# One score bank per block of an attention kernel exponentiated on GpSimd by pow instead of on ScalarE

## The chip, the cores and the metric

One core of one Trainium2 chip. The metric is the device time of one execution in microseconds. Before: 530.76 us, median of 2 runs (530.7 to 530.82); in later jobs on other chips the same kernel took 527.4 to 533.3, so single runs here carry about half a per cent of noise. A kernel is compared with runs of the kernel before on the same chip; each run also has a state, and only fast runs are compared, except where a kernel had a single run, whose state is unknown.

## The reference, cut to what matters

```python
xn = layernorm(x)                                  # x: 1 x 2048 x 448, bf16
q, k, v = split(xn @ wqkv)                         # 16 heads of 28
p = softmax(q @ k.T * 28 ** -0.5)
s = (p @ v) @ wo
g = silu(gelu(xn @ w1 + b1) @ w2 + b2)
return x + s * g
```

16 heads x 2048 x 2048 scores have to be exponentiated. That is the largest work outside TensorE.

## The kernel before

A small scheduler written in Python places every instruction with an assumed duration and emits one in-order program per engine; semaphores carry the dependences. Scores are made in 16 blocks (4 groups of heads x 4 chunks of queries) of 64 banks of 128x512. Three banks (two in the first block) are exponentiated by one ScalarE instruction. PSUM is where the matmuls of this kernel put their results, SBUF where everything else lies; a bank is one 128x512 tile of scores in PSUM.

```python
UB = 3; NRING = 6; NP = 21
...
def fexp(eng, b0=b0, p0=p0, n=n):                  # p_exps, ScalarE (L932)
    return eng.activation(K.P[:, p0:p0 + n, :], K.ring[:, b0:b0 + n, :], ACTF.Exp, scale=SM_SCALE)
...
# p_pv, TensorE (L969): P and the values, summed over the 64 banks of a block in one PSUM bank
eng.matmul(K.acc[32 * j:32 * j + 32, ...], K.vaug[:, t, 4 * g + j, :], K.P[:, PB[m], ...], ...)
...
# p_silu, VectorE (L871): two SBUF inputs
eng.scalar_tensor_tensor(K.g_sb[:, c, t, :], sg[:, t, :], 1.0, fb[:, t, :], op0=ALU.add, op1=ALU.mult)
```

The ring has six PSUM banks, that is, two units of three: TensorE fills one while ScalarE reads the other. `acc` holds one block at a time, so every bank of a block must have been multiplied in before the block can be closed, some 28.6 us (64/3 x 1.343) after it began.

Of the kernel before, what the change touches and what calls it, by code (L numbers as in the profile page):

```python
# [8 lines left out]
ALU = mybir.AluOpType  # L9
ET = mybir.EngineType  # L10

PE, ACT, DVE, POOL, SP = ET.PE, ET.Activation, ET.DVE, ET.Pool, ET.SP

S = 2048
D = 448
# [12 lines left out]
NBLK = G * C  # L28
MTOT = NBLK * T * 4

UNITS = []
for _m in range(0, 64, 2):
    UNITS.append(([_m, _m + 1], _m % 4, _m % 20))
for _m in range(64, MTOT, UB):
    UNITS.append((list(range(_m, _m + UB)), (_m - 64) % NRING, (_m - 64) % NP))
NU = len(UNITS)
RB = {m: b0 + k for ms, b0, p0 in UNITS for k, m in enumerate(ms)}
PB = {m: p0 + k for ms, b0, p0 in UNITS for k, m in enumerate(ms)}
SM_SCALE = DH ** -0.5
LN_EPS = 1e-5  # L40
KNORM = 2.5
PV_START = 8
SEM = 0.07
EPS = 0.1

# [23 lines left out]
class _Kernel:  # L69
# [19 lines left out]
    def sb(self, name, shape, dtype=dt.bfloat16):  # L89
        return self.es.enter_context(self.nc.sbuf_tensor(name, shape, dtype))  # L90
# [143 lines left out]
    def alloc(self):  # L234
# [57 lines left out]
        self.b_acc, self.b_misc = B(), B()  # L292
        self.b_P = [B() for _ in range(NP)]
        self.b_x = [B() for _ in range(C)]
        self.b_xn = [[B() for _ in range(4)] for _ in range(3)]
        self.b_xnT = [[B(), B()] for _ in range(C)]
        self.b_wqkf = B()
# [24 lines left out]
        self.b_rf = [B(), B()]  # L322
        self.banks = [(self.misc[:, :], self.b_misc), (self.acc[:, :], self.b_acc)]
        self.s_x = [self.sem("s_x%d" % q) for q in range(4)]
        self.s_out = [self.sem("s_out%d" % q) for q in range(10)]
        self.s_w = {n: self.sem("s_" + n) for n in ("wqk", "wv", "w1", "w2", "wo", "b")}

    def schedule(self):
        K = self
        K.n_f1 = 0  # L330
        K.exp_u = -1
        K.sc_u = -1
        K.pv_u = -1
        K.E_done = -1
        K.norms_done = False
        K.stg_done = 0
        K.qsqs = [0, 1]
        K.f2n = [0] * C
        K.pv_started = False
        K.chunks_done = 0  # L340
        K.g_done = [False] * C
        K.on_done = [False] * NBLK
        K.on4 = [False] * 4
        K.ln_done = 0
        K.ring6 = False
        K.taken = 0
        K.ring_busy = [False] * NRING
        K.P_busy = [False] * NP
        K.banks += [(K.ring[:, b, :], K.b_ring[b]) for b in (5, 4)]
        K.outs = []  # L350
        K.b1_done = False
        K.gelu_done = False
        self.constants()
        self.loads()
        for c in range(C):
            K.spawn(K.p_ln(c), c)
        K.spawn(K.p_first(), 0)
        K.spawn(K.p_scores(), 0)
        K.spawn(K.p_take(4), 0)
        K.spawn(K.p_take(5), 0)  # L360
        K.spawn(K.p_exps(), 0)
        K.spawn(K.p_pv(), 0)
        o = 1.0

        def nxt():
            nonlocal o
            o += 1.0
            return o
        K.spawn(K.p_norms(), nxt())
        for c in range(1, C):  # L370
            K.spawn(K.p_tr(c, 0), nxt())
            K.spawn(K.p_tr(c, 1), nxt())
            K.spawn(K.p_k(0, c), nxt())
            if c == 1:
                K.spawn(K.p_v0(0), nxt())
            K.spawn(K.p_v0(c), nxt())
        K.spawn(K.p_q(0, 1), nxt())
        for c in (2, 3):
            K.spawn(K.p_q(0, c), nxt())
        for c in range(C):  # L380
            K.spawn(K.p_k(1, c), nxt())
        K.spawn(K.p_q(1, 0), nxt())
        for t in range(T):
            K.spawn(K.p_v1(t), nxt())
        for c in (1, 2, 3):
            K.spawn(K.p_q(1, c), nxt())
        f1 = deque((c, ft) for c in range(C) for ft in range(FT))
        for c in range(C):
            for _ in range(6):
                K.spawn(K.p_f1(*f1.popleft()), nxt())  # L390
            K.spawn(K.p_k(2, c), nxt())
            K.spawn(K.p_q(2, c), nxt())
        while f1:
            K.spawn(K.p_f1(*f1.popleft()), nxt())
        for c in range(C):
            K.spawn(K.p_k(3, c), nxt())
            K.spawn(K.p_q(3, c), nxt())
        K.spawn(K.p_gelu(), 0)
        for c in range(C):
            for t in range(4):  # L400
                K.spawn(K.p_f2(c, t), nxt())
            K.spawn(K.p_silu(c), nxt())
        K.o_epi = 0.5
        for c in range(C - 1):
            for t in range(4):
                K.spawn(K.p_out(c, t), nxt())
        for t in range(4):
            K.spawn(K.p_last(t), nxt())
        K.run()
        for h in K.outs:  # L410
            K.wait(SP, h)

    def constants(self):
# [3 lines left out]
        def f(eng):  # L417
            eng.memset(K.epsc[:, :], LN_EPS)
            eng.memset(K.dum[:, :], 1.0)
            eng.memset(K.ones[:, :], 1.0)  # L420
            eng.memset(K.E_sb[:, :, :], 0.0)
            eng.memset(K.w1[64:128, 3, :], 0.0)
            eng.memset(K.stg[64:128, 3, :, :, :], 0.0)
            pad = lambda w: w.rearrange("p k (h e) -> p (k h) e", e=32)[:, :, DH:32]
            eng.memset(pad(K.wq[:, :, :]), 0.0)
            eng.memset(pad(K.wk[:, :, :]), 0.0)
            eng.memset(pad(K.wsq), 0.0)
            eng.memset(K.wv[64:128, 3, :], 0.0)
            eng.memset(K.wv[0:64, 3, D:WS], 0.0)
            eng.memset(K.wv[:, 0:3, D:WS], 0.0)  # L430
            return eng.memset(K.xn[:, :, :, D:512], 0.0)
# [432 lines left out]
    def p_silu(self, c):  # L864
        K = self
        yield ("until", lambda: K.f2n[c] == 4 and K.ready([K.b_fsb[c % 2]], 0.3) and (c < 2 or K.g_done[c - 2]))
        fb, sg = K.fsb[:, c % 2, :, :], K.sig[:, c % 2, :, :]
        yield _Task(ACT, lambda eng: eng.activation(sg, fb, ACTF.Tanh, scale=0.5),
                    [K.b_fsb[c % 2]], [K.b_sig[c % 2]], 1.6, 0.0, 0)
        for t in range(4):  # L870
            yield _Task(DVE, lambda eng, t=t: eng.scalar_tensor_tensor(K.g_sb[:, c, t, :], sg[:, t, :], 1.0, fb[:, t, :],  # L871
                                                                       op0=ALU.add, op1=ALU.mult),
                        [K.b_sig[c % 2], K.b_fsb[c % 2]], [K.b_h[c], K.b_g[c]], 0.63, 0.0, 6)
        K.g_done[c] = True

    def pieces(self, m):
        b, r = m // 64, m % 64
# [11 lines left out]
    def p_scores(self):  # L889
        K = self  # L890
        for u in range(NU):
# [23 lines left out]
            if len(ms) == 3 and not K.ring6:  # L915
                yield ("until", lambda: K.taken == 2)
                K.ring6 = True
            yield ("until", lambda: not any(K.ring_busy[RB[m]] for m in ms))
            yield _Task(PE, fall, rd, [K.b_ring[RB[m]] for m in ms], 0.17 + 0.05 * len(ms) + 0.02 * (len(fl) - len(ms)), 0.1, 1)
            for m in ms:  # L920
                K.ring_busy[RB[m]] = True
            K.sc_u = u

    def p_exps(self):
        K = self
        for u in range(NU):
            ms, b0, p0 = UNITS[u]
            n = len(ms)
            yield ("until", lambda: K.sc_u >= u and not any(K.P_busy[p0 + k] for k in range(n)))

            def fexp(eng, b0=b0, p0=p0, n=n):
                return eng.activation(K.P[:, p0:p0 + n, :], K.ring[:, b0:b0 + n, :], ACTF.Exp, scale=SM_SCALE)  # L932
            yield _Task(ACT, fexp, [K.b_ring[b0 + k] for k in range(n)], [K.b_P[p0 + k] for k in range(n)],
                        0.0843 + 0.4267 * n, 0.08, 3)
            for k in range(n):
                K.ring_busy[b0 + k] = False
                K.P_busy[p0 + k] = True
            K.exp_u = u
            if u >= NU - 2:
                for k in range(n):  # L940
                    K.banks.append((K.ring[:, b0 + k, :], K.b_ring[b0 + k]))

    def p_pv(self):
        K = self
# [2 lines left out]
        K.banks.pop(i)  # L947
        K.pv_started = True
        for u in range(NU):
            ms = UNITS[u][0]  # L950
            parts, cur = [], []
            for m in ms:
                cur.append(m)
# [4 lines left out]
            for part in parts:  # L958
                if not part:
                    continue  # L960
                first = K.sub_of(part[0])
                yield ("until", lambda: K.exp_u >= u and K.E_done >= first - 1)
                fl, rd = [], []
                for m in part:
                    b, j, pc, end, s = K.pieces(m)
# [15 lines left out]
                yield _Task(PE, fall, rd, [K.b_acc], 0.18 + 0.05 * len(part) + 0.02 * (len(fl) - len(part)), 0.1,  # L981
                            lambda: 1.2 if K.exp_u - K.pv_u > 4 else 6)
                for m in part:
                    K.P_busy[PB[m]] = False
                if end:
                    K.spawn(K.p_epi(b) if b < NBLK - 1 else K.p_epi4(s), 0.5)
            K.pv_u = u
# [72 lines left out]
    def t_oev(self, ps, tok, c, t):  # L1060
# [2 lines left out]
        wr = K.b_osb[c][t // 2] if c < C - 1 else K.b_o4[t]  # L1063
        yield _Task(DVE, lambda eng: eng.tensor_tensor(o, ps, K.g_sb[:, c, t, :], ALU.mult),  # L1064
                    [tok, K.b_g[c]], [wr], 0.63, 0.0, 3)
        yield _Task(DVE, lambda eng: eng.tensor_tensor(o, o, K.x_sb[:, c, t, :], ALU.add),
                    [K.b_x[c], wr], [wr], 0.4, 0.0, 3)
        ov = K.out[0].rearrange("(c p t) d -> c p t d", p=128, t=4)[c]
        if c == C - 1:
            K.outs.append(K.dma(SP, lambda eng: eng.dma_start(ov[:, t, :], o), K.s_out[6 + t], reads=[wr]))  # L1070
# [75 lines left out]
```

## Time and profile before

| | before |
|---|---|
| time | 530.76 us |
| ScalarE busy | 502.8 us, 95% |
| TensorE busy | 466.3 us, 88% |
| GpSimd busy | 64.1 us, 12% |
| pitch of a three-bank exponential | 1.343 us |

### The profile page before, as it was taken

How to read it: one execution, taken by the hardware profiler on the slowest of the kernel's cores; microseconds unless marked ns; L12 is line 12 of the kernel's file. 1: busy time of each engine (PE TensorE's matmuls, PEld its weight loads, DVE VectorE, ACT ScalarE, POOL GpSimd, SP SyncE). 2: the span in 40 equal slices, each digit the busy share in tenths (PEclk: the TensorE clock that was granted, in tenths of full speed). 3: DMA queues.
4: the chain of work that ended last, by engine and by line, in shares of the span. 5: the costliest groups of instructions: out<-in, count | busy, mean ns of one | idle time of the engine just before them, and what ended most of it. 6: DMA issues, size and time to landing. Idle time of an engine off the chain costs nothing.

```text
span 529.0 us, 8343 instructions
## 1 busy us (share of the span) xinstructions
PE 466.3 (88%) x3478; PEld 149.9 (28%) x3507; DVE 172.5 (33%) x304; ACT 502.8 (95%) x385; POOL 64.1 (12%) x93
## 2 busy tenths in 40 slices
PE   6899899899989999989976799999878889898984
PEld 2433233222222222222221333333212112121542
DVE  6823433343433343343433132313400003031244
ACT  3898999999999999999999799999999999999993
POOL 5662101210101001010111001000101000010100
PEclk9999999999999999999995999999955558566698
DMA  8800000000000000000000000000000000000010
GB/s 238 245 16 18 0 1 1 0 1 1 1 1 1 0 1 2 1 1 1 0 1 0 0 2 1 1 0 1 1 0 2 0 1 35 1 14 22 2 46 27
DMA packets 7925, 9.13 MB, mean 17 GB/s; under 512 B 2384, under 2 KB 6928, under 8 KB 7888
## 3 DMA queue, kind: packets, MB, share of 16 engines
q1 hardware_dynamic: 7888, 8.61, 5.3%
q8 instruction: 27, 0.44, 0.3%
q14 instruction: 10, 0.08, 0.0%
HBM read 6.77 MB, written 1.84 MB: 16 GB/s over the span
## 4 chain that ended last, share of the span: by engine, by line
ACT 44%; PE 36%; issue 14%; DVE 5%; ACTq 0%; DVEq 0%
ACT P L932 44%; PE ring L903 8%; PE misc L854 8%; PE acc L969 7%; PE misc L591 3%; PE misc L1055 2%; PE acc L678 2%; PE misc L771 1%; PE misc L1040 1%; DVE h L1064 1%; DVE qT L747 1%; PE misc L811 1%; DVE qT L757 1%; DVE h L871 1%; PE ring L591 1%
## 5 line engine op out<-in xcount | busy, mean ns | idle before, releaser
L932 ACT ACTIVATE P<-ring 128x1536 bf16<-128x1536 f32 (+1 forms) x352 | 461.8, 1644 | 7.3 <-PE ring L903 4.7
L903 PE MATMUL ring<-qT,kT 32*128 32x512 bf16 (+1 forms) x1216 | 151.4, 386 | 31.7 <-ACT P L932 29.2
L969 PE MATMUL acc<-P,vaug 128*32 128x512 bf16 (+1 forms) x1216 | 145.5, 390 | 0.0
L903 PEld LDWEIGHTS ring<-qT,kT 32*128 32x128 bf16 x1216 | 38.1, 94 | 156.6 <-ACT P L932 132.0
L824 DVE TENSOR_SCALAR h<-misc,b1c 128x512 bf16<-128x512 f32 x56 | 42.0, 751 | 80.4 <-PE misc L811 80.4
L811 PE MATMUL misc<-xnT,w 128*128 128x512 bf16 x209 | 58.8, 382 | 3.3 <-issue 1.3
L969 PEld LDWEIGHTS acc<-P,vaug 128*32 128x32 bf16 x1216 | 35.6, 96 | 83.5 <-issue 80.6
L854 PE MATMUL misc<-w,h 128*128 128x448 bf16 x224 | 52.5, 362 | 3.7 <-DVE qT L757 2.0
L1030 POOL CAST rhi<-rc 128x512 bf16<-128x512 f32 x15 | 9.1, 609 | 306.6 <-DVE rc L1026 223.8
L1016 DVE CAST E_sb<-acc 128x512 bf16<-128x512 f32 x15 | 10.3, 687 | 79.6 <-PE acc L969 79.6
L752 POOL TENSOR_TENSOR qsq<-qT 128x512 bf16<-128x512 bf16 x15 | 15.6, 1039 | 113.1 <-DVE qT L747 113.1
L859 DVE TENSOR_TENSOR w<-misc,b2b 128x448 bf16<-128x448 f32 x16 | 10.0, 622 | 54.3 <-PE misc L854 54.3
L854 PEld LDWEIGHTS misc<-w,h 128*128 128x128 bf16 x224 | 18.1, 99 | 28.4 <-issue 11.3
L836 ACT ACTIVATE h<-h 128x7168 bf16<-128x7168 bf16 x4 | 24.4, 6163 | 0.0
L811 PEld LDWEIGHTS misc<-xnT,w 128*128 128x128 bf16 x224 | 15.5, 97 | 30.2 <-issue 9.6
L591 PE MATMUL misc<-xnT,wq 128*128 128x512 bf16 x53 | 15.7, 418 | 3.0 <-DVE qT L757 2.5
L591 PE MATMUL misc<-xnT,wk 128*128 128x512 bf16 x47 | 14.9, 424 | 3.9 <-DVE qT L747 2.8
L1045 DVE TENSOR_TENSOR qT<-misc,E_sb 128x512 bf16<-128x512 f32 x15 | 10.4, 691 | 21.4 <-PE misc L1040 21.4
L747 DVE CAST qT<-misc 128x512 bf16<-128x512 f32 x14 | 9.7, 691 | 20.2 <-PE misc L591 20.2
L1031 POOL TENSOR_TENSOR rlo<-rc,rhi 128x512 bf16<-128x512 f32 x15 | 16.0, 1064 | 1.2
L602 DVE TENSOR_SCALAR kT<-misc,ecol 128x512 bf16<-128x512 f32 x13 | 9.8, 750 | 19.3 <-PE misc L591 19.3
L1055 PE MATMUL misc<-wo,qT 128*128 128x448 bf16 x56 | 15.1, 371 | 0.8 <-DVE w L1004 0.4
(119 smaller groups left out, 245.7 us busy)
## 6 DMA issues: line engine op xcount, KB each, us to landing
x_sb<-in_A_x_dram SPq DMA_DIRECT2D x4, 448.0 KB, 6.7
w<-in_B_w_dram SPq DMA_DIRECT2D x1, 1568.0 KB, 13.0
w<-in_B_w_dram SPq DMA_DIRECT2D x1, 1344.0 KB, 7.5
out_dram<-h SPq DMA_DIRECT2D x6, 224.0 KB, 2.0
h<-in_A_wqkv_dram SPq DMA_DIRECT2D x1, 672.0 KB, 4.8
out_dram<-h SPq DMA_DIRECT2D x4, 112.0 KB, 1.7
wo<-in_A_wo_dram SPq DMA_DIRECT2D x16, 24.5 KB
wv<-in_A_wqkv_dram SPq DMA_DIRECT2D x1, 336.0 KB, 5.7
```

The lines of the kernel that those rows point to most:

```text
L591: ins = eng.matmul(bank, w[:, kt, g * 128:(g + 1) * 128], K.xnT[:, kt, c * 512:(c + 1) * 512], start=(kt == 0), stop=(kt == KT - 1))
L747: yield _Task(DVE, lambda eng: eng.tensor_copy(qb, bank), [tok], [qr], 0.7, 0.0, 2)
L752: yield _Task(POOL, lambda eng: eng.tensor_tensor(qs, qb, qb, ALU.mult), [qr], [tq], 1.05, 0.0, 0)
L811: ins = eng.matmul(bank, K.w1[:, kt, ft * 128:(ft + 1) * 128], K.xnT[:, kt, c * 512:(c + 1) * 512], start=(kt == 0), stop=(kt == KT - 1))
L824: yield _Task(DVE, lambda eng: eng.tensor_scalar(dst, bank, K.b1c[:, ft:ft + 1], None, op0=ALU.add), [tok, K.b_b1c], wr, 0.75, 0.0, 2)
L836: return eng.activation(hv, hv, ACTF.Gelu_apprx_tanh)
L854: ins = eng.matmul(ps, hv[:, ft, t * 128:(t + 1) * 128], K.w2[:, ft, :], start=(ft == 0), stop=(ft == FT - 1))
L903: return eng.matmul(K.ring[:, RB[m], col:col + nq], K.kT[32 * j:32 * j + 32, g, t * 128:(t + 1) * 128], K.qT[32 * j:32 * j + 32, g, c * 51 ...
L932: return eng.activation(K.P[:, p0:p0 + n, :], K.ring[:, b0:b0 + n, :], ACTF.Exp, scale=SM_SCALE)
L969: return eng.matmul(K.acc[32 * j:32 * j + 32, q0:q0 + nq], K.vaug[:, t, 4 * g + j, :], K.P[:, PB[m], col:col + nq], tile_position=(0, 32 * ...
L1031: yield _Task(En, lambda eng: eng.tensor_tensor(K.rlo[:, :, :], rcb, K.rhi[:, :, :], ALU.subtract), [K.b_rc, K.b_rhl], [K.b_rhl], d2, 0.0, 1)
L1055: ins = eng.matmul(ps, K.qT[:, g, c * 512 + t * 128:c * 512 + (t + 1) * 128], K.wo[:, g, :], start=(g == 0), stop=(g == G - 1))
```

## The change

The intent: GpSimd is idle for 88% of the time, and ScalarE is the bound, so one bank of each of the blocks 1 to 14 goes to GpSimd. VectorE first copies the bank, scaled by the softmax scale times log2(e), from PSUM to SBUF in fp32; GpSimd then computes two to the power of it from SBUF. The late bank's matmul is a task of its own, to be placed when the pow has ended. The space of x holds the copies, so x is loaded again for the residual at the end. The core of the diff, cut:

```diff
+LATE = {}
+for _b in range(1, NBLK - 1):
+    for _r in (8,):
+        _m = 64 * _b + _r
+        while (_m - 64) % UB != UB - 1:
+            _m += 1
+        LATE[_m] = POOL
...
+POW_DUR = 20.0
...
+    yield _Task(DVE, lambda eng, m=m, i=i: eng.tensor_scalar(K.ysb[i], K.ring[:, RB[m], :], SM_SCALE * LOG2E,
+                                                             None, op0=ALU.mult), ..., 0.72, 0.0, 1)
...
+    yield _Task(POOL, lambda eng: eng.tensor_tensor(K.plate[k], K.two[:, 0:1].to_broadcast([128, 512]), K.ysb[i],
+                                                    ALU.pow), [K.b_y[i], K.b_pads], [K.b_pl[k]], POW_DUR, 0.0, 2)
...
+    yield ("until", lambda: K.pv_done[64 * b + 3] and K.ready([K.b_pl[k]], 0.1))
+    yield _Task(PE, lambda eng: eng.matmul(K.acc[32 * j:32 * j + 32, :], K.vaug[:, t, 4 * g + j, :], K.plate[k], ...
...
-        yield _Task(DVE, lambda eng: eng.tensor_tensor(o, o, K.x_sb[:, c, t, :], ALU.add),
+        yield _Task(DVE, lambda eng: eng.tensor_tensor(o, o, K.x2[:, c, t, :], ALU.add),
```

In the changed kernel the pow is L998, the scaled copy L988, the late matmul L1004, the exponentials L966, the silu product L904.

More of the change, by code (lines that the diff above doesn't have):

```diff
@@ L29 @@
 MTOT = NBLK * T * 4
-UNITS = []
-for _m in range(0, 64, 2):
-    UNITS.append(([_m, _m + 1], _m % 4, _m % 20))
-for _m in range(64, MTOT, UB):
-    UNITS.append((list(range(_m, _m + UB)), (_m - 64) % NRING, (_m - 64) % NP))
+LATE = {}
[5 more added lines that the diff above has]
+        LATE[_m] = POOL
+UNITS, RB, PB, RPREV, PPREV = [], {}, {}, {}, {}
+_last, _plast, _p = {}, {}, 0
+for _m in list(range(0, 64, 2)) + list(range(64, MTOT, UB)):
+    _ms = list(range(_m, _m + (2 if _m < 64 else UB)))
+    _b0 = _m % 4 if _m < 64 else (_m - 64) % NRING
+    _na = len([m for m in _ms if m not in LATE])
+    if _p + _na > NP:
+        _p = 0
+    UNITS.append((_ms, _ms[:_na], _b0, _p))
+    for _k, m in enumerate(_ms):
+        RB[m] = _b0 + _k
+        RPREV[m] = _last.get(RB[m])
+        _last[RB[m]] = m
+        if _k < _na:
+            PB[m] = _p + _k
+            PPREV[m] = _plast.get(PB[m])
+            _plast[PB[m]] = m
+    _p += _na
 NU = len(UNITS)
-RB = {m: b0 + k for ms, b0, p0 in UNITS for k, m in enumerate(ms)}
-PB = {m: p0 + k for ms, b0, p0 in UNITS for k, m in enumerate(ms)}
 SM_SCALE = DH ** -0.5
+LOG2E = 1.4426950408889634
 LN_EPS = 1e-5
@@ L294, in alloc @@
         self.b_x = [B() for _ in range(C)]
+        self.b_x2 = [B() for _ in range(C)]
+        xf = self.x_sb[:, :, :, :].rearrange("p c t d -> p (c t d)")
+        self.ysb = [xf[:, 1024 * i:1024 * (i + 1)].bitcast(f32) for i in range(2)]
+        self.plate = [xf[:, 2048 + 512 * i:2560 + 512 * i] for i in range(2)]
+        self.x2 = self.h[:, :, 3584:5376].rearrange("p c (t d) -> p c t d", d=D)
+        self.b_y, self.b_pl = [B(), B()], [B(), B()]
+        self.two = sb("two", [128, 1], f32)
         self.b_xn = [[B() for _ in range(4)] for _ in range(3)]
@@ L324, in alloc @@
         self.s_x = [self.sem("s_x%d" % q) for q in range(4)]
+        self.s_x2 = [self.sem("s_x2%d" % q) for q in range(4)]
         self.s_out = [self.sem("s_out%d" % q) for q in range(10)]
@@ L346, in schedule @@
         K.taken = 0
-        K.ring_busy = [False] * NRING
-        K.P_busy = [False] * NP
+        K.ring_rel = [False] * MTOT
+        K.pv_done = [False] * MTOT
+        K.late_left = [len([m for m in LATE if m // 64 == b]) for b in range(NBLK)]
+        K.ys, K.pls = [0, 1], [0, 1]
         K.banks += [(K.ring[:, b, :], K.b_ring[b]) for b in (5, 4)]
@@ L362, in schedule @@
         K.spawn(K.p_pv(), 0)
+        K.spawn(K.p_late(), 0)
         o = 1.0
@@ L419, in f @@
             eng.memset(K.dum[:, :], 1.0)
+            eng.memset(K.two[:, :], 2.0)
             eng.memset(K.ones[:, :], 1.0)
@@ L874, in p_silu @@
         K.g_done[c] = True
+        K.b_x2[c].r = list(K.b_h[c].r) + [K.b_h[c].w]
+        K.dma(SP, lambda eng: eng.dma_start(K.x2[:, c, :, :], K.A_x[0].rearrange("(c p t) d -> c p t d", p=128, t=4)[c]),
+              K.s_x2[c], writes=[K.b_x2[c]])
     def pieces(self, m):
@@ L917, in p_scores @@
                 K.ring6 = True
-            yield ("until", lambda: not any(K.ring_busy[RB[m]] for m in ms))
+            yield ("until", lambda: all(RPREV[m] is None or K.ring_rel[RPREV[m]] for m in ms))
             yield _Task(PE, fall, rd, [K.b_ring[RB[m]] for m in ms], 0.17 + 0.05 * len(ms) + 0.02 * (len(fl) - len(ms)), 0.1, 1)
-            for m in ms:
-                K.ring_busy[RB[m]] = True
             K.sc_u = u
@@ L926, in p_exps @@
         for u in range(NU):
-            ms, b0, p0 = UNITS[u]
+            _, ms, b0, p0 = UNITS[u]
             n = len(ms)
-            yield ("until", lambda: K.sc_u >= u and not any(K.P_busy[p0 + k] for k in range(n)))
+            yield ("until", lambda: K.sc_u >= u and all(PPREV[m] is None or K.pv_done[PPREV[m]] for m in ms))
             def fexp(eng, b0=b0, p0=p0, n=n):
@@ L934, in p_exps @@
                         0.0843 + 0.4267 * n, 0.08, 3)
-            for k in range(n):
-                K.ring_busy[b0 + k] = False
-                K.P_busy[p0 + k] = True
+            for m in ms:
+                K.ring_rel[m] = True
             K.exp_u = u
@@ L941, in p_exps, with p_late, p_pow @@
                     K.banks.append((K.ring[:, b0 + k, :], K.b_ring[b0 + k]))
+    def p_late(self):
+        K = self
+        yield ("until", lambda: K.ln_done == 2 * C)
+        for b in K.b_y + K.b_pl:
+            for x in K.b_x:
+                b.r += x.r
+        for u in range(NU):
+            for m in UNITS[u][0]:
+                if m not in LATE:
+                    continue
+                yield ("until", lambda: K.sc_u >= u and len(K.ys) > 0)
+                i = K.ys.pop(0)
+                yield _Task(DVE, lambda eng, m=m, i=i: eng.tensor_scalar(K.ysb[i], K.ring[:, RB[m], :], SM_SCALE * LOG2E,
+                                                                         None, op0=ALU.mult),
+                            [K.b_ring[RB[m]]], [K.b_y[i]], 0.72, 0.0, 1)
+                K.ring_rel[m] = True
+                K.spawn(K.p_pow(m, i), 0)
+    def p_pow(self, m, i):
+        K = self
+        yield ("until", lambda: len(K.pls) > 0)
+        k = K.pls.pop(0)
+        yield _Task(POOL, lambda eng: eng.tensor_tensor(K.plate[k], K.two[:, 0:1].to_broadcast([128, 512]), K.ysb[i],
+                                                        ALU.pow), [K.b_y[i], K.b_pads], [K.b_pl[k]], POW_DUR, 0.0, 2)
+        K.ys.append(i)
+        b, j, pc, end, s = K.pieces(m)
+        g, t = b // C, pc[0][0]
+        yield ("until", lambda: K.pv_done[64 * b + 3] and K.ready([K.b_pl[k]], 0.1))
+        yield _Task(PE, lambda eng: eng.matmul(K.acc[32 * j:32 * j + 32, :], K.vaug[:, t, 4 * g + j, :], K.plate[k],
+                                               tile_position=(0, 32 * j), start=False, stop=False, skip_group_check=True),
+                    [K.b_pl[k], K.b_v[0 if g == 0 else 1][t]], [K.b_acc], 0.25, 0.1, 1.2)
+        K.pls.append(k)
+        K.late_left[b] -= 1
     def p_pv(self):
@@ L949, in p_pv @@
         for u in range(NU):
-            ms = UNITS[u][0]
+            ms = UNITS[u][1]
             parts, cur = [], []
@@ L961, in p_pv @@
                 first = K.sub_of(part[0])
-                yield ("until", lambda: K.exp_u >= u and K.E_done >= first - 1)
+                yield ("until", lambda: K.exp_u >= u and K.E_done >= first - 1 and (
+                    not K.pieces(part[-1])[3] or K.late_left[part[-1] // 64] == 0))
                 fl, rd = [], []
@@ L983, in p_pv @@
                 for m in part:
-                    K.P_busy[PB[m]] = False
+                    K.pv_done[m] = True
                 if end:
@@ L1065, in t_oev @@
                     [tok, K.b_g[c]], [wr], 0.63, 0.0, 3)
-        yield _Task(DVE, lambda eng: eng.tensor_tensor(o, o, K.x_sb[:, c, t, :], ALU.add),
-                    [K.b_x[c], wr], [wr], 0.4, 0.0, 3)
+        yield _Task(DVE, lambda eng: eng.tensor_tensor(o, o, K.x2[:, c, t, :], ALU.add),
+                    [K.b_x2[c], wr], [wr], 0.4, 0.0, 3)
         ov = K.out[0].rearrange("(c p t) d -> c p t d", p=128, t=4)[c]
```

## The prediction

> **What bounds the kernel now.** I read the page first: shares of engines, slices, chain of waits, then the groups by shape, then ScalarE's exponentials in windows of 20 us.
>
> ```profile
> PE 466.3 (88%) x3478; PEld 149.9 (28%) x3507; DVE 172.5 (33%) x304; ACT 502.8 (95%) x385; POOL 64.1 (12%) x93
> ...
> ACT 44%; PE 36%; issue 14%; DVE 5%; ACTq 0%; DVEq 0%
> ```
>
> ScalarE is 95% busy, and the missing 5% is mostly the start (9.52 us busy in the first 20). GpSimd is 88% idle; that is what the change wants to use. TensorE at 88% is not far behind, so I ask next whether the exponentials really stand back to back.
>
> ```profile
> L932 ACT ACTIVATE P<-ring 128x1536 bf16<-128x1536 f32 x320 | 431.7, 1706 | 6.8 <-PE ring L903 4.4 <-PE acc L969 2.1
> L932 ACT ACTIVATE P<-ring 128x1024 bf16<-128x1024 f32 x32 | 30.1, 1028 | 0.4 <-PE ring L903 0.3
> ```
>
> These are groups by shape: 320 exponentials of three banks in 431.7 us busy, 1.349 us each, 32 of two banks in 30.1 us, 0.941 each. The mean of 1706 ns is longer than the pitch because neighbours overlap. The idle time before them is 7 us in all. From end to end of single exponentials in the trace I get 1.343 us for three banks (299 of 320) and 0.917 for two: one bank is worth 0.426 us.
>
> ```profile
> 240.00:260.00 20.00, 20.00 (x16) 1.00 0.00 1
> ...
> 300.00:320.00 20.00, 16.52 (x13) 1.00 0.01 1
> 320.00:340.00 20.00, 18.45 (x15) 1.00 0.00 1
> ...
> 400.00:420.00 20.00, 19.92 (x16) 0.50 0.00 1
> ```
>
> These are windows of the exponentials alone (ScalarE busy, granted TensorE clock). They fill ScalarE from 60 us to the Gelu and again to 520 us, even where the clock is 0.50. The whole engine view of 320 to 340 us has TensorE busy 19.86 of 20 us: in the stage of the second MLP matmul (L854, 296 to 378 us) TensorE has no spare time, so time that it loses there is not made up.
>
> **What the Trainium skill says.** (1) "ScalarE: Activation LUTs", section "What ACT_TABLE_LOAD costs", gives 0.833 ns per element; 512 elements are 0.427 us. The trace agrees, 0.426. (2) "GPSIMD Engine Reference", section 3.1, gives about 2.6 cycles per element for a two-input tensor_tensor, an estimate of 1.1 us for 512 at 1.2 GHz; the trace has 1.04 to 1.06 us for such ones (L752, L1031). It has no figure for pow. (3) "SBUF — State Buffer", section "Who interferes with whom", says that VectorE and GpSimd share a port pair as an exclusive lock for the whole instruction, and that a VectorE instruction with two SBUF inputs contends with a GpSimd one that reads SBUF; with at most one SBUF input and outside the 2-port modes it does not. This decides my prediction, so I looked for it in the trace before:
>
> ```profile
> 379.95 3.47 DVE L871 SCALAR_TENSOR_TENSOR h<-w 128x448 bf16<-128x448 bf16 x4 [0.38 <-ACT w L868]
> ...
> 379.63 0.61 POOL L1030 CAST rhi<-rc 128x512 bf16<-128x512 f32 x1 [22.15 <-PE acc L969]
> 380.32 1.30 POOL L1031 TENSOR_TENSOR rlo<-rc,rhi 128x512 bf16<-128x512 f32 x1
> ```
>
> L871 (silu's product, two SBUF inputs) takes 624 ns in the median. Here four take 3.47 us, about 0.9 too long. Singly: where one overlapped a GpSimd instruction it ended 0.48 us after that one's end, three times of three (380.24 to 380.72, 381.63 to 382.11, 357.48 to 357.96), and lasted up to 1.35 us. And L1031 took 1.30 instead of 1.05. VectorE instructions with a PSUM input (L757 beside L752, L824 beside L1031) keep their 0.75 us. So the trace agrees with the lock. (4) "TensorE: Matmul & The Clock Gate", Part 1, has the array at half clock after an idle window of about 3.4 us. The trace shows 0.5 during Gelu, from 276.5 to 293.6 us.
>
> **The change part by part.**
> Removed: in each of blocks 1 to 14 one three-bank exponential becomes a two-bank one. 14 x 0.426 = 6.0 us less on ScalarE, all of it on the path if ScalarE stays fed. That alone gives 530.8 - 6.0 = 524.8 us.
> Added on VectorE: 14 scaled copies PSUM to SBUF, some 0.75 us each like L824, 10.5 us on an engine that is 33% busy. It frees the ring's bank about when the exponential would have. Off the path.
> Added on GpSimd: 14 pows of 128x512. No trace has one. The diff's scheduling constant says 20.0 us, and the other constants of that table fit the trace (0.75 against 751 ns, 1.05 against 1064), so I take 20 as an estimate. 280 us on an idle engine, one pow per block of about 28.6 us (64/3 x 1.343).
> Moved: the matmul of the late bank. In the order of TensorE's instructions it stands 46 to 49 score banks after the bank it belongs to, mostly 49: 16.3 units x 1.343 = 21.9 us; less score matmul, copy and hand-overs (0.4 + 0.75 + 0.2) about 20.6 us are left for pow. That just fits.
> The reload of x is 4 DMAs of 448 KB when the queues are nearly empty (6.7 us each at the start): hidden.
>
> **What the pow locks.** Over its 20 us any VectorE instruction with two SBUF inputs waits, and VectorE takes its work in order. After the first pow those are L871 (16, now L904) and the residual add L1066 (16, now L1134). I placed them by the order of instructions:
> - Silu of chunk 0: ScalarE's order is the two-bank exponential, 3 exponentials, the Tanh (1.741), so the product comes 0.92 + 3 x 1.343 + 1.74 = 6.7 us after pow began. VectorE stands until 20. Behind it waits the eviction of the only free bank (L859, now L892). TensorE stands 7 score groups after the late bank's at a matmul for that bank; ScalarE is fed for 0.92 + 7 x 1.343 + 1.74 = 12.1 us. It resumes at 20 + 0.48 + 3 x 0.66 (rest of the four products) + 0.62 (eviction) + about 1.4 (matmuls, score, hand-over) = 24.5. Idle 12.4 us.
> - Silu of chunk 1: the products stand right behind the scaled copy and one eviction (0.69), so pow begins first and they wait some 19.3 us. TensorE has two more score groups, then the row sums' matmul waits for the eviction behind three products. pow begins about 1.2 us before the two-bank exponential here (its copy runs while one exponential is still to come). ScalarE is fed for 1.2 + 0.92 + 2.69 = 4.8 us and resumes at 20 + 0.48 + 2 x 0.66 + 0.62 + 0.8 = 23.2. Idle 18.4 us.
> - Chunk 2: its Tanh is 14 exponentials after the two-bank one, about 20 us: nothing. Chunk 3: 7 exponentials after, blocked some 8 us, but TensorE needs nothing of VectorE there: nothing.
> - Residual adds: one of chunk 0 stands just behind the last scaled copy and should win the race; the next waits some 17 us, with only pow's own successors behind it: an output DMA later, no more.
> Sum: 12.4 + 18.4 = 30.8 us of new ScalarE idle. After each stall the clock may need a window to come back; at half speed in a stage without slack I estimate 1 us each, 2 in all. 530.8 - 6.0 + 30.8 + 2 = 557.6; I say 557.
>
> **Rivals.**
> (a) No lock that matters: pow takes its operand early, or releases the port between pieces. Then 524.8 to 527, the wish of the change. Against it speak the three waits above, but they are of instructions of 1 us, not of 20.
> (b) pow's length is not 20. Each us less takes 2 us from the stalls (15 us: about 547; 10 us: about 536, as only stalls of the second kind are left in full). Each us over about 21.5 (20.6 and the one exponential that is in the ring) stalls TensorE at the late matmul in most of the 14 blocks: at 23 us some 20 us more, at 25 us over 600 in all.
> (c) TensorE's half clock from 380 us on eats the gain: 400 to 440 us still shows 16 exponentials per 20 us at clock 0.50, so at most 1 to 2 us of the 6 are lost.
> (d) GpSimd's normalisation (rhi, rlo) and squares of q queue behind pow: their consumers on TensorE stand 3 to 5 units after the late matmul, some 4 to 6 us for 1.7 to 2.7 us of work. No wait of its own.
>
> **Range and chances.** I give the lock with pow near 20 about 65%: 550 to 570. A pow clearly shorter, with the lock, 10%: 530 to 548. A longer pow 8%: above 570. No lock that matters 17%: 524 to 528. So 526 to 575 should hold it 8 times in 10. Within 2% (520.1 to 541.4) is rival (a) and half of the short pow: 0.23. Faster by over 2% would need more than the 6 us that are removed: 0.01. Slower: 0.76.
>
> **What would show it.** Right: pows of about 20 us; two exponentials with 12 and 18 us of idle before them in the second MLP stage, released by TensorE, TensorE by VectorE; the first of a group of silu products lasting 13 and 19 us and ending 0.5 us after a pow; two-bank exponentials elsewhere at 0.92 us pitch with no gap. Wrong: products of 0.62 us inside a pow (no lock), or gaps at the late matmul once per block (pow too long), or a gap at the silu products that is made up later.

## More of the kernel before

The prediction shows the lines behind the table. Two more are needed to compare with later. First the view of waits of the kernel before (who waited for whom: us in total, times, longest):

```profile
PEld ring L903 <- ACT P L932: 132.0, 265, 1.8
...
ACT P L932 <- PE ring L903: 4.7, 6, 2.9
```

The weight loads of TensorE's score matmuls (PEld) wait for ScalarE to free the ring 265 times; the exponentials wait for scores only 6 times, 4.7 us. That is the signature of a kernel whose bound is ScalarE. And from the page, the busy tenths in 40 slices of the span:

```profile
ACT  3898999999999999999999799999999999999993
POOL 5662101210101001010111001000101000010100
```

## The result, and the profile after

1408.6 us (1408.02 and 1409.18), against 530.76: a ratio of 2.654, 95% interval 2.643 to 2.665. A ratio here is the mean time of one kernel's fast runs over that of the other's fast runs of the same rounds, so not quite the ratio of the medians quoted. The time lies far outside the predicted 526 to 575 us.

From the page of the changed kernel, the shares, the slices of ScalarE and GpSimd, the chain that ended last, and the groups of the pow and of the late matmul:

```profile
PE 483.2 (34%) x3477; PEld 151.3 (11%) x3507; DVE 179.1 (13%) x319; ACT 500.2 (36%) x385; POOL 1210.0 (86%) x107
...
ACT  7910704307025061070391080260530803407017
...
POOL 6599898998979989989799369799699798997980
...
POOL 82%; PE 10%; issue 4%; ACT 2%; DVE 2%; POOLq 0%; DVEq 0%; ACTq 0%
...
L998 POOL TENSOR_TENSOR x_sb<-two,x_sb 128x512 bf16<-128x512 f32 x14 | 1147.0, 81926 | 109.2 <-DVE x_sb L988 75.4
...
L1004 PE MATMUL acc<-x_sb,vaug 128*32 128x512 bf16 x14 | 8.5, 608 | 866.2 <-POOL x_sb L998 866.2
```

One line tells it: 14 pows of 81.93 us each. The busy time of ScalarE hardly moved (502.8 to 500.2); it is spread over a longer span, and the slices show it: full stretches became a pattern of work and holes. The chain of waits, 44% ScalarE before, is now 82% GpSimd.

The view of waits, after:

```profile
ACT P L966 <- PE ring L939: 886.5, 35, 68.4
...
PE acc L1004 <- POOL x_sb L998: 866.2, 14, 62.6
...
PEld ring L939 <- ACT P L966: 110.7, 222, 2.5
```

The exponentials' wait for scores went from 4.7 to 886.5 us, and TensorE's wait for the pow is 866.2 us in exactly 14 waits, 61.9 each. While the late matmul waits, no score matmul behind it runs, the ring empties, and ScalarE stops. TensorE's timeline over one such wait, two rows that follow one another:

```profile
255.63 0.40 PE L1037 MATMUL acc<-P,vaug 128*32 128x512 bf16 x3
318.31 0.61 PE L1004 MATMUL acc<-x_sb,vaug 128*32 128x512 bf16 x1 [62.28 <-POOL x_sb L998]
```

No other order of instructions could have saved this version: 14 pows of 81.92 us keep GpSimd busy for 1147 us, more than twice the time of the kernel before.

A window of the changed kernel over one pow, all engines (columns: stretch, its length, then busy us of TensorE, weight loads, VectorE, ScalarE and GpSimd with counts, clock, DMA):

```profile
1010.00:1100.00 90.00, 23.00 (x171) 7.04 (x169) 6.39 (x11) 28.37 (x21) 83.08 (x3) 0.61 0.02 6
```

28.4 us of ScalarE's work per 90 us: a block lasts as long as its pow and some 9 us more, and nothing else of the program fills the rest.

And the lock of the prediction? The timeline of the changed kernel for GpSimd and VectorE around two pows:

```profile
821.43 81.92 POOL L998 TENSOR_TENSOR x_sb<-two,x_sb 128x512 bf16<-128x512 f32 x1 [15.34 <-DVE x_sb L988]
...
827.97 2.60 DVE L904 SCALAR_TENSOR_TENSOR h<-w 128x448 bf16<-128x448 bf16 x4 [1.32 <-ACT w L901]
...
914.34 81.92 POOL L998 TENSOR_TENSOR x_sb<-two,x_sb 128x512 bf16<-128x512 f32 x1 [9.30 <-PE misc L887]
914.78 2.40 DVE L904 SCALAR_TENSOR_TENSOR h<-w 128x448 bf16<-128x448 bf16 x3
```

Four silu products 6.5 us into a pow take 2.60 us, 0.65 each: no wait at all. Of the three that were issued 0.44 us after the next pow began, the first lasted 1.085 us, the others 0.62. Of the 15 products that were issued inside a pow one alone was held, by less than half a microsecond.

### The profile page after: what moved, and what is told of

The parts are those of the page before. It is cut to its first block, busy times and chain, and to the rows that moved or that the text cites. A ratio compares the mean times of both kernels' runs of the same rounds, so it can differ in the third digit from the quotient of the medians.

```text
span 1407.4 us, 8383 instructions
## 1 busy us (share of the span) xinstructions
PE 483.2 (34%) x3477; PEld 151.3 (11%) x3507; DVE 179.1 (13%) x319; ACT 500.2 (36%) x385; POOL 1210.0 (86%) x107
## 4 chain that ended last, share of the span: by engine, by line
POOL 82%; PE 10%; issue 4%; ACT 2%; DVE 2%; POOLq 0%; DVEq 0%; ACTq 0%
POOL x_sb L998 81%; ACT P L966 2%; PE ring L939 2%; PE misc L887 2%; PE acc L1037 2%; PE misc L624 1%; PE acc L711 1%; PE misc L1108 1%; PE misc L844 0%; PE acc L1004 0%; DVE qT L790 0%; POOL rlo L1099 0%; PE misc L787 0%; PE misc L804 0%; DVE qT L780 0%
## 5 line engine op out<-in xcount | busy, mean ns | idle before, releaser
L998 POOL TENSOR_TENSOR x_sb<-two,x_sb 128x512 bf16<-128x512 f32 x14 | 1147.0, 81926 | 109.2 <-DVE x_sb L988 75.4
L966 ACT ACTIVATE P<-ring 128x1536 bf16<-128x1536 f32 (+1 forms) x352 | 459.2, 1456 | 887.0 <-PE ring L939 886.5
L1004 PE MATMUL acc<-x_sb,vaug 128*32 128x512 bf16 x14 | 8.5, 608 | 866.2 <-POOL x_sb L998 866.2
L1004 PEld LDWEIGHTS acc<-x_sb,vaug 128*32 128x32 bf16 x14 | 1.4, 100 | 871.3 <-POOL x_sb L998 871.3
L844 PE MATMUL misc<-xnT,w 128*128 128x512 bf16 x206 | 62.1, 404 | 4.0 <-issue 2.9
L887 PE MATMUL misc<-w,h 128*128 128x448 bf16 x224 | 55.5, 375 | 2.9 <-DVE qT L790 2.0
L1113 DVE TENSOR_TENSOR qT<-misc,E_sb 128x512 bf16<-128x512 f32 x15 | 10.4, 692 | 330.9 <-PE misc L1108 330.9
L814 DVE CAST vaug<-misc 128x336 bf16<-128x336 f32 x16 | 8.1, 506 | 78.8 <-PE misc L804 78.8
```

The lines of the kernel that those rows point to most:

```text
L844: ins = eng.matmul(bank, K.w1[:, kt, ft * 128:(ft + 1) * 128], K.xnT[:, kt, c * 512:(c + 1) * 512], start=(kt == 0), stop=(kt == KT - 1))
L887: ins = eng.matmul(ps, hv[:, ft, t * 128:(t + 1) * 128], K.w2[:, ft, :], start=(ft == 0), stop=(ft == FT - 1))
L998: yield _Task(POOL, lambda eng: eng.tensor_tensor(K.plate[k], K.two[:, 0:1].to_broadcast([128, 512]), K.ysb[i], ALU.pow), [K.b_y[i], K.b_p ...
```

## The experiments

Theory A: the length of the pow is the whole loss; it has a fixed price per element, and what exceeds the slot that the order of instructions leaves is lost 14 times. Rivals: other parts of the change cost a share (copies, late matmul, reload, lock); the price is per instruction or depends on the values; the schedule itself was unsound. The first five runs have the order of instructions of the changed kernel; in the others the scheduler places the instructions anew.

A word on "right result": the comparison with the reference passed the multiplication and the zero exponents below, which compute no exponential for those banks. It therefore says little about the weights of 14 banks in 1024; where I call a result right, that is by the formula.

**A multiplication in the place of the pow**

```diff
-  ... K.two[:, 0:1].to_broadcast([128, 512]), K.ysb[i], ALU.pow)
+  ... K.two[:, 0:1].to_broadcast([128, 512]), K.ysb[i], ALU.mult)
```

> The pow is replaced by a multiplication of the same two operands, same shapes, same order of all instructions (the result is wrong on purpose). Theory A, that the length of the pow alone is the whole loss: this GpSimd instruction takes about 1.05 us, no wait at the late matmul is left, and the time is that of before less 14 x 0.426 us of ScalarE: 524 to 527 us. Theory B, that something else in the change (the scaled copies on VectorE, the late matmul as a task of its own, the reload of x, the port lock) costs a share of it: the time stays clearly above 531 us.

Measured: 526.05 us (523.98 to 526.89, 4 runs) against 531.39; ratio 0.9877, interval 0.9835 to 0.9919. The group of the instruction in this run:

```profile
L998 POOL TENSOR_TENSOR x_sb<-two,x_sb x14: 1038/1039/1117, 52.5 to 461.6; 128x512 bf16<-128x512 f32 x14
```

Minimum, median and maximum of its duration are 1.04 to 1.12 us, against 81.92 for the same operands with pow. So theory A holds as to what is lost, and the rest of the change delivers its 6 us: 1.2% of 530.8 is 6.5 (by the interval 4.3 to 8.8). This run also gives the slot without a pow that could stretch it: from the start of the GpSimd instruction to its late matmul pass 19.58 to 21.00 us, 20.2 in the middle; less the 0.05 us from the end of a pow to the waiting matmul, about 20.1 are left for the instruction.

**Half of the bank**

```diff
-  eng.tensor_tensor(K.plate[k], K.two[:, 0:1].to_broadcast([128, 512]), K.ysb[i], ALU.pow)
+  eng.tensor_tensor(K.plate[k][:, 0:256], K.two[:, 0:1].to_broadcast([128, 256]), K.ysb[i][:, 0:256], ALU.pow)
```

> The pow works on 256 of the 512 columns of the bank (the other half of the copy is stale: wrong result on purpose). Theory A, a price per element of 160 ns: the pow takes 41.0 us, and each of the 14 waits at the late matmul is 41.0 - 20.6 = 20.4 us or up to 1.5 us less: 524.8 + 14 x 20 = about 800 us. Rival, a price that is mostly fixed per instruction: the pow stays near 80 us and the time near 1400. For the port lock: the silu product that is issued 0.4 us after a pow began waits until about 0.5 us after its start if the lock ends with the reading of the operand, and hardly waits; if the lock had a fixed length of about 1 us, it waits as in the full pow (1.08 us long).

Measured: 837.33 us (one run, state unknown; wrong result, as meant). The pow and who waited for it:

```profile
L998 POOL TENSOR_TENSOR x_sb<-two,x_sb x14: 41115/41116/41194, 52.0 to 751.2; 128x256 bf16<-128x256 f32 x14
...
  PE acc L1004: 294.6, 14
```

41.1 us, half of 81.9: a price per element. The 14 waits are 21.0 us each, 41.1 less 20.1, without the 1.5 us of grace that I had allowed for. That makes 524.8 + 14 x 21.0 = 819 us and not 800; the other 18 us are taken up below. The silu product issued 0.43 us after a pow's start lasted 0.658 us, against 1.085 at full width: the lock is shorter with a shorter operand.

**A quarter of the bank: the pow at the length that was planned**

The same edit with 128 in place of 256.

> The pow works on 128 of 512 columns (wrong result on purpose), so that it takes about the 20 us for which the schedule was made. Theory A: pow of 20.5 us, no wait at the late matmul of over 0.5 us, silu products inside a pow at 0.62 us: 524 to 528 us, that is, the schedule of the change was sound and only the length of the instruction was wrong. Rival, the lock of the prediction: two waits of 12 and 18 us, about 557 us.

Measured: 534.49 us (533.8 to 535.17, 4 fast runs), ratio 1.0049, interval 1.0017 to 1.0081. No product waited (0.615 to 0.626 us, all 16), so the rival of the lock falls. But the expected 524 to 528 is missed as well:

```profile
L998 POOL TENSOR_TENSOR x_sb<-two,x_sb x14: 20715/20716/20792, 52.9 to 469.0; 128x128 bf16<-128x128 f32 x14
...
  PE acc L1004: 9.0, 12
```

The pow takes 20.72 us and the slot is 20.1: TensorE waits in 12 blocks of 14, 9.0 us in all. 14 x (20.72 - 20.1) = 8.7 us, and this run is 534.49 - 526.05 = 8.4 us above the multiplication on the same chip. So the schedule had no slack: at 3.6% above the length that it assumed the change has already lost its whole gain.

**96 columns: a pow that fits**

The same edit with 96.

> The pow works on 96 columns (wrong result on purpose): by the 159.4 ns per element of the three lengths measured it takes 96 x 0.1594 + 0.3 = 15.6 us, well within the 19.6 to 21.0 us that the order of instructions leaves for it. Theory A: no wait at the late matmul, and the time of the multiplication in its place, 0.985 to 0.99 of before (about 525 to 526 us); then the 8 us between 128 columns and the multiplication are the overrun of 0.6 us, 14 times, and not the pow as such. Rival, a running pow costs other engines something all along (port lock, shared power or clock): a time between the two.

Measured: 525.48 us (523.78 to 526.36, 4 fast runs) against 528.63; ratio 0.9916, interval 0.9875 to 0.9957. In the view of the instruction's waiters nothing is listed, and

```profile
L998 POOL TENSOR_TENSOR x_sb<-two,x_sb x14: 15615/15616/15693, 52.3 to 458.7; 128x96 bf16<-128x96 f32 x14
```

15.6 us, as computed from the other widths. The interval overlaps that of the multiplication, so a running pow as such costs nothing that these runs can resolve (the two were compared on different chips, each with the kernel before); a fraction of a per cent stays possible.

**Exponents of zero**

```diff
-  eng.tensor_scalar(K.ysb[i], K.ring[:, RB[m], :], SM_SCALE * LOG2E, None, op0=ALU.mult)
+  eng.tensor_scalar(K.ysb[i], K.ring[:, RB[m], :], 0.0, None, op0=ALU.mult)
```

> The scaled copy multiplies by zero, so every exponent is 0 and every result 1 (wrong result on purpose); all else as in the changed kernel. Theory A, a routine of fixed length per element: pow 81.9 us, time 1400 to 1415. Rival, a routine with branches or steps that depend on the value: another length of the pow, and a time that moves by 14 times the difference.

Measured: 1406.75 us (one run); the pow took 81.915 to 81.993 us, as before to the last few ns. The length does not depend on these values.

**One block alone**

```diff
-for _b in range(1, NBLK - 1):
+for _b in (4,):
```

Blocks are counted from 0, so this is the fifth.

> Only one block (the fourth) gives a bank to GpSimd by the full pow; the other 13 are as before, and the result is right. Theory A, each pow is paid for by itself: one pow of 81.9 us, one wait at the late matmul of 62 us, nothing else moves: 530.8 + 62 - 0.4 = about 592 us. Rival, a cost of having GpSimd, the copies and the reloaded x at all, whatever the number of blocks: well above 592.

Measured: 594.24 us (one run, state unknown) against 528.63. One pow of 81.95 us, one wait of 61.8 us at the late matmul. 65.6 us for a wait of 61.8: the 4 us between them are near the spread of the runs of before in that job (528.1 to 531.7), and a single run does not settle them.

**The exponential from cheap GpSimd instructions**

The runs say that a plain GpSimd tensor_tensor of this size costs 1.04 us and the slot is 20. So up to some 18 plain instructions may replace the pow. I took exp(z) = ((1 + u + u^2/2) e^(-a/64))^64 with u = (z + a)/64 and a = 10.4, since with these inputs the exponents lie about 10.4 below zero in the mean. VectorE's copy gives u + 1; squaring, one scale-and-add (1 + u + u^2/2 is half of (1+u)^2 + 1) and six squarings follow:

```diff
+NSQ = 6; Z0 = 10.4; KSQ = 0.5 * 2.718281828459045 ** (-Z0 / 2 ** NSQ)
...
-  ... SM_SCALE * LOG2E, None, op0=ALU.mult)
+  ... SM_SCALE / 2 ** NSQ, 1.0 + Z0 / 2 ** NSQ, op0=ALU.mult, op1=ALU.add)
-  yield _Task(POOL, ... ALU.pow ...)
+  y = K.ysb[i]
+  for n in range(NSQ + 1):
+      d, db = (K.plate[k], K.b_pl[k]) if n == NSQ else (y, K.b_y[i])
+      yield _Task(POOL, lambda eng, d=d: eng.tensor_tensor(d, y, y, ALU.mult), [K.b_y[i]], [db], 1.12, 0.0, 2)
+      if n == 0:
+          yield _Task(POOL, lambda eng: eng.tensor_scalar(y, y, KSQ, KSQ, op0=ALU.mult, op1=ALU.add), ...)
```

By arithmetic off the chip on sampled exponents of the reference's inputs the weights are off by 0.05% in the root mean square, and by up to 2.5% for the rarest exponents (0.2% and 11% with the five squarings used at the end). The constant a fits these inputs; exponents far from it would need range handling.

> The pow is replaced by eight GpSimd instructions that give the exponential by a second-order start and six squarings (right result, relative error of a weight in the mean 0.04%). By the 1.04 us of one GpSimd tensor_tensor of this size in the run with a multiplication each takes 0.8 to 1.1 us, some 8.5 us for a bank, inside the slot of 20 us: no wait at the late matmul, time as with the multiplication, 0.985 to 0.99 of before. Rival, the port lock of two-input instructions now counts, as eight instructions read SBUF one after the other: silu products and residual adds wait up to 1 us each, at most some 5 us in the stage without slack.

Measured: 526.02 us in the median of 4 runs, but two of them were slow; ratio of the fast ones 0.9856, interval 0.9795 to 0.9916. Again, with more rounds:

> One bank per block again, with more rounds on the same chip as two and three banks: 0.988, the 6.0 us.

Measured: 525.09 us (523.03 to 529.38, 6 fast runs) against 530.76; ratio 0.992, interval 0.9869 to 0.9971. As the multiplication, within noise. The rival has a small share: the silu products of this run last 0.85 us in the mean against 0.71 before, some 2 us over all 16.

**Two banks per block**, `for _r in (8, 29)`:

> The same with two banks per block, 28 in all: 28 x 0.426 = 11.9 us less on ScalarE, GpSimd busy some 17 of 28 us per block. If ScalarE stays the bound: 0.975 to 0.98 of before, some 518 to 520 us. If TensorE, which is nearly full in the second MLP stage and at half clock in the last third, becomes the bound: 0.98 to 0.99, little better than one bank.

Measured: 522.57 us (4 fast runs) against 528.63; ratio 0.9874, interval 0.9826 to 0.9923. Again:

> Two banks per block again, with more rounds, since one and two banks could not be told apart: 0.977 if ScalarE alone sets the time, 0.987 if the second bank gains nothing.

Measured: 522.8 us (6 fast runs) against 530.76; ratio 0.9872, interval 0.9837 to 0.9908. Only 6.8 us of the 11.9 arrive.

**Three banks per block**, `for _r in (8, 23, 38)`, five squarings instead of six:

> Three banks per block, 42 in all, by five squarings each (seven GpSimd instructions, some 7.3 us a bank; weights off by 0.2% in the mean). 42 x 0.426 = 17.9 us less on ScalarE. If ScalarE stays the bound: 0.966 of before, about 513 us. If TensorE holds it in the second MLP stage and at half clock in the last third: about 0.98, no better than one or two banks.

Measured: 516.52 us (515.76 to 518.37, 6 fast runs) against 530.76; ratio 0.9748, interval 0.9716 to 0.978. This version beats the kernel before by 2.5%, clear of noise, and so the changed one by far. Its shares from the page, then three of its groups by shape (the squarings, the two-bank exponentials, the scale-and-add):

```profile
PE 456.0 (89%) x3478; PEld 148.3 (29%) x3507; DVE 207.1 (40%) x347; ACT 486.4 (95%) x385; POOL 349.7 (68%) x387
```

```profile
L1003 POOL TENSOR_TENSOR x_sb<-x_sb 128x512 f32<-128x512 f32 x210 | 219.3, 1055 | 79.2 <-DVE x_sb L990 73.0 <-PE misc L889 0.2
...
L968 ACT ACTIVATE P<-ring 128x1024 bf16<-128x1024 f32 x74 | 79.3, 1109 | 2.6 <-PE ring L941 2.4
...
L1005 POOL TENSOR_SCALAR x_sb<-x_sb 128x512 f32<-128x512 f32 x42 | 26.2, 623 | 1.2
```

Squarings of 1.055 us and one step of 0.62: six of the first (the start and five) and one of the second come to 7.0 us a bank by their recorded spans, against 81.9 by pow. GpSimd is 68% busy and ScalarE still 95%. ScalarE's exponentials fell by 16.5 us (461.8 to 445.3 busy), the time by 13.4 (2.52% of 530.76). The windows of the exponentials over the second MLP stage show where some of it stays, first before, then with three banks (ScalarE busy with exponentials, of 80 us):

```profile
300.00:380.00 80.00, 72.20 (x54) 1.00 0.00 1
```

```profile
300.00:380.00 80.00, 67.59 (x52) 0.97 0.04 12
```

There the exponentials take up less of the same stretch than before, so ScalarE waits more. TensorE did not become fuller: in the view of all engines it is busy for 78.6 of these 80 us before and for 74.8 with three banks. The longest of the new waits, in the timeline of all engines, has another cause:

```profile
347.54 4.10 DVE L906 SCALAR_TENSOR_TENSOR h<-w 128x448 bf16<-128x448 bf16 x3
...
352.23 1.67 PE L889 MATMUL misc<-w,h 128*128 128x448 bf16 x4 [2.37 <-DVE w L894]
...
354.49 1.45 ACT L968 ACTIVATE P<-ring 128x1536 bf16<-128x1536 f32 x1 [2.96 <-PE ring L941]
```

Silu products that meet the squarings on GpSimd take 1.3 us each instead of 0.62; the eviction behind them (L894) comes late, TensorE waits 2.4 us for it, and ScalarE 3.0 us for TensorE. Over all 16, a product lasts 1.07 us in the mean against 0.71 before. So the port lock of short GpSimd instructions, the rival named for one bank, reaches the critical path here. How much of the missing 4.5 us (17.9 less 13.4) it explains, and why two banks got 57% of what they took off ScalarE and three got 75%, I did not separate.

## Why the prediction was wrong, point by point

- **ScalarE is the bound, and 6.0 us are on its path: right.** The multiplication in the pow's place gained 1.2%, 6.5 us of 530.8. One reading on the way was loose: after the Gelu the exponentials do not fill ScalarE at once. It is busy for 17.99 us of 300 to 320 with the Tanh counted, and one gap of 2.9 us stands at 299.
- **The copies, the late matmul and the reload of x cost nothing: right, as far as that run resolves.** In it the reloads landed in 3.3 us each.
- **"so I take 20 as an estimate": wrong, and this is the step that failed.** The mechanism behind rival (b) was the right one, its size was not. A pow of 128x512 takes 81.92 us, not 20.0, so "That just fits" became 14 waits of 61.9 us at the late matmul, 866 us in all. I had taken it from a planning constant of the kernel's author, and trusted it because its neighbours in the table agreed with the trace; but those were of instructions that the trace had, and this one was of an instruction that no trace had. The round figure was the warning. I gave a longer pow 8%. That I forecast "slower" with 0.76 was luck: nearly all of it rested on the lock, which held one product here by less than half a microsecond.
- **A slot of "about 20.6 us": off by 0.5.** The run without a long pow shows 20.1. Small, but it is the difference between gaining 6 us and losing 3, as the quarter bank shows.
- **"Each us over about 21.5 ... stalls": the threshold is the slot itself.** I had counted on one exponential in the ring as grace. The waits at 512, 256 and 128 columns are 61.9, 21.0 and 0.64 us in the mean over 14 blocks: pow less 20.1 gives 61.8, 21.0 and 0.6. With the measured length the prediction's own sum gives 524.8 + 14 x (81.92 - 20.1) = 1390 us; measured 1408.6. ScalarE's idle gaps of over 0.3 us before exponentials sum to 885 us instead of 6, some 19 more than the 866 of the 14 waits. The 14 long holes are 874 us, 8 more than the waits, and after 12 of them a second hole of 0.6 to 1.6 us follows, 10 us in all. In the trace the granted clock is 0.50 at the end of every long wait and for at least 3.3 us after it. At half width the excess is as large (18 us), so it goes with the number of the waits and not with their length; how much of it is clock I did not separate.
- **30.8 us by the port lock: wrong, a second step that failed.** The prediction let the lock last for the whole pow, which the section that it cites does not say of two SBUF inputs. The lock exists, but it was shorter: a product 0.44 us into a pow ended 1.52 us after the pow's start, that is, about 1.04 us plus the 0.48 us that such a product needs after a release; later ones ran freely. 1.04 us is what a whole GpSimd tensor_tensor of these operands takes, and in the run with the multiplication the product in the same place lasted 1.082 us, against 1.085 in the pow: a pow held the port no longer than a multiplication that was over in 1.04 us. With the pow of 20.72 us no product waited and the time was 534.49 us, so 557 would have been wrong even with the right length. The three waits that I had found before fit both readings, since reading and instruction ended together there; I noted that they were of short instructions, and still gave the lock 75%.
- **Rivals (c) and (d)** (half clock, normalisation behind pow): no run was made for them alone; with a short instruction in the pow's place there is no loss left for them to explain.

## What to carry to other kernels

A duration that no trace had was nearly the whole loss here: before planning an offload around one, run the instruction once by itself, or at two sizes, and read its price per element. A late operand stopped everything behind its consumer on TensorE, so an offloaded result needs slack in its slot, not a slot of just its length; here 3% over the slot, 14 times, turned a gain of 6 us into a loss of 3. And an idle engine is of use for what it does cheaply: seven plain GpSimd instructions gave these exponentials, to about 0.2%, in a twelfth of the time of one pow.

## What the Trainium skill lacked or had wrong

- "GPSIMD Engine Reference" has no cost for pow. Measured at four widths (96, 128, 256 and 512 columns: 15.616, 20.716, 41.116 and 81.917 us, fp32 in, bf16 out, base by broadcast): 0.1594 us per column plus 0.3 us, the same for exponents that are all zero. A multiplication of the same operands took 1.04 us, so the figure in its section 3.1 for plain two-input instructions (an estimate of 1.1 us from it, in the prediction) fits, and must not be carried over to pow.
- "SBUF — State Buffer", section "Who interferes with whom", says that a VectorE instruction with two SBUF inputs contends with a GpSimd instruction that reads SBUF, but not for how long; that the shared pair is held for the whole instruction it says of VectorE's 2-port modes. Here such instructions were held to the end of short GpSimd instructions, but only until about 1.04 us after the start of an 81.9 us pow, less long at half width (a product of 0.658 us), not at all at a quarter; 14 of the 15 products issued inside a full pow ran at 0.61 to 0.63 us. The reading of the operand, not the instruction, seems to be what holds the port; that is inferred from these lengths.
- "Perfetto Trace Analysis", section "GPSIMD Engine Instruction", says to treat the span of a GpSimd instruction in a hardware profile as unreliable. Here the recorded ends of the pows held: in all 14 blocks the waiting matmul started 0.05 to 0.06 us after the end of its pow. Of the short instructions the spans are a little long: squarings in a row start 1.00 us apart in the three-bank run and are recorded with 1.055.
